# Buffer slots handed out by age, weight splits made one by one, and two small matmuls moved, in a kernel of attention and a feed-forward block

## The chip, the core and the metric

The kernel runs on one core of a Trainium2 chip. The time is that of one execution on the device, in microseconds (us). Engines are named as the profile names them: PE (TensorE, matmuls), PEld (its weight loads), ACT (ScalarE), DVE (VectorE), POOL (GpSimd), and SP, whose queue issues the DMAs.

## The reference

```
xn = layernorm(x)                       # x: 2048 x 512
q, k, v = split(xn @ wqkv)              # 32 heads of 16
p = softmax(q k^T / 4, keys at most 255 behind the query)
s = (p v) @ wo
h = silu(xn @ w1) * (xn @ w3)           # 1792 columns
out = x + s * silu(h @ w2)
```

All inputs and the output are fp32.

## The kernel before, in words

**Precision.** Every dense fp32 product is made of fp16 matmuls. An operand is scaled and split into a high half and a low half (`hi`, `lo`), and a product is the sum of hi·hi, hi·lo and lo·hi. A weight matrix is split in steps: `squares` (L170 on) takes a sum of squares of each part on ACT (`sqa`, L178) or DVE (`sqd`, L180) and casts the sums to `sb` (L190); `powers` multiplies `sb` with ones on PE (L203) and makes a power of two from it on DVE (L205 to L210); the split itself scales the raw weights on ACT (L227), casts the high half on ACT (L228), and subtracts on POOL (L224, in two halves).

**Tiles.** The 2048 tokens are four tiles of 512. For each tile, 4 blocks of 128 tokens are loaded (L317), get their statistics on DVE (bn_stats and bn_aggr, L321 and L322; a 1/sqrt by Newton steps, L326 to L336), are normalised (L339) and transposed on PE (L355) with copies on ACT and DVE (L358, L363).

**Attention.** There are 16 pairs of tile and group of 8 heads, each in two units, so 32 units. `project` makes q or k of a group (L423), `value` makes v (L393). A q or k goes through DRAM (`dQ`, `dK`, L439 to L443) to be fetched in another layout (L455). Pass 1 of a unit (L476 on PE, L481 on DVE) finds the row maxima; they go through DRAM into two more rows of `qa` (L492 to L499). Pass 2 makes the scores (L523), adds masks on DVE (L532, L537), takes the exp on ACT (L541) and multiplies with v (L551). The scores of both passes lie in `s`, two PSUM buffers, so PE can write the next only when DVE or ACT has read the last. `normalise` divides by the sums: POOL multiplies with `rb`, ACT casts the result `O` (L595), POOL subtracts.

**Feed-forward.** F = 1792 is 14 blocks of 128, in four groups. `gate_up` makes the gate and up products of a block (L684), with a tanh on ACT (L695), two products on DVE (L699, L704), and a split of the result `hh` into halves (L708 on ACT, then POOL). `down` (L729) multiplies a group with w2 and adds to an accumulator on DVE (L745). `total` joins attention and feed-forward (sigmoid by a tanh, L765; product L766; output projection L771; store L780). For the first tile the weights are loaded raw (L619 to L621), measured in pairs of blocks (`measure`), split, used, and stored split (`dW1` at L689, `dW2` at L732); the later tiles load the stored halves (L613 to L615).

**What sets the order.** PE's instructions run in the order in which the program emits them; those of the other engines and of SP are ordered by a scheduler that starts from the emission, in which `urgent()` puts softmax work first. The emission is a walk through pieces of dense work: `spread` mixes a unit's batches of attention with dense pieces, and after each piece `step()` raises the count `now` and runs what `later(n, f)` has queued for that count. So `later(4, scale)` is four pieces on. Each engine then runs its instructions in its order, and one that waits holds all behind it.

**Slots.** 32 buffers of SBUF hold raw weights, split weights, q and k on their way, tiles of x, `hh`, accumulators and outputs. `take` pops the first name of a list and `give` appends to its end, when the last use has been emitted. The new user of a slot waits for the last reader of the old one: a matmul, a POOL subtraction, or a DMA that stores it.

The change lies in `take` and `give`, in `measure` and `measure_down`, and in the `give` calls of `project`, `gate_up` and `total`.

Of the kernel before, what the change touches and what calls it, by code (L numbers as in the profile page):

```python
# [11 lines left out]
F16 = mybir.dt.float16  # L12
# [10 lines left out]
D = 512  # L23
# [27 lines left out]
SLOTS = 32  # L51
# [13 lines left out]
def tile_block(ctx: ExitStack, tc: tile.TileContext, x, wqkv, wo, w1, w3, w2, out):  # L65
# [20 lines left out]
    pso = pool("pso", 1, PSUM)  # L86


    free = [f"slot{i}" for i in range(SLOTS)]
    held = {}  # L90

    def take(dtype):
        slot = free.pop(0)
        made = fpool.tile([P, 512 if dtype == F32 else 1024], dtype, name=slot, tag=slot, bufs=1)
        held[id(made)] = slot, made
        return made

    def give(*tiles):
        for made in tiles:
            free.append(held.pop(id(made))[0])  # L100

    queue = []
    now = [0]
    started = []

    def urgent():
# [5 lines left out]
    def later(n, f):  # L115
        made_so_far[0] += 1
        queue.append((now[0] + n, made_so_far[0], f))
# [103 lines left out]
    def halves(op, out, a, b):  # L221

        for c in (slice(0, 256), slice(256, 512)):
            op(out[:, c], a[:, c], b[:, c])  # L224

    def split_pool(hi, lo, raw, s):
        nc.scalar.activation(raw, raw, AF.Copy, scale=s)  # L227
        nc.scalar.copy(hi, raw)  # L228
        halves(nc.gpsimd.tensor_sub, lo, raw, hi)
# [177 lines left out]
    def project(t, g, k, terms=(range(3),)):  # L407


        cell = {}  # L410

        parts = ([[(c, i) for c in (2 * half, 2 * half + 1) for i in range(3)] for half in range(2)] if len(terms) == 1
                 else [[(c, i) for i in group for c in range(NC)] for group in terms])

        def part(n):
            assert turned[t] == 4
            hi, lo, _ = WQK[g]
            xh, xl = X[t]
            if n == 0:
                cell["pp"] = psm.tile([P, TW], F32, name="mm", tag="mm")  # L420
            for c, i in parts[n]:
                a, b = ((hi, xh), (lo, xh), (hi, xl))[i]
                nc.tensor.matmul(cell["pp"], a[:, k, c, :], b[:, c, :], start=(c, i) == parts[0][0],  # L423
                                 stop=(c, i) == parts[-1][-1])
            if n < len(parts) - 1:
                return
            pp = cell["pp"]
            both = take(F16)
            B = both.rearrange("p (a t) -> p a t", a=2)
            s = QS / (XS * WS)  # L430
            with urgent():
                nc.scalar.activation(B[:, 0, :], pp, AF.Copy, scale=s)

            def rest():
                with urgent():
                    nc.vector.scalar_tensor_tensor(B[:, 1, :], pp, s, B[:, 0, :], op0=ALU.mult, op1=ALU.subtract)
                d = (dQ, dK)[k][g][:, :, t * TW:(t + 1) * TW]
                if k == 0:
                    nc.sync.dma_start(d[:, 0:2, :], B[:, 0:1, :].to_broadcast([P, 2, TW]))  # L439
                    nc.sync.dma_start(d[:, 2, :], B[:, 1, :])  # L440
                else:
                    nc.sync.dma_start(d[:, 0:2, :], B)
                    nc.sync.dma_start(d[:, 2, :], B[:, 0, :])  # L443
                give(both)
            later(1, rest)
        return [(len(l), lambda n=n: part(n)) for n, l in enumerate(parts)]

# [155 lines left out]
    WF = {}  # L603
# [21 lines left out]
    def measure(f, apart=0):  # L625

        raws = [RAW[f + i][0] for i in range(2)]
        sb = squares([raws[0][0], raws[1][0], raws[0][1], raws[1][1], RAW[f][1], RAW[f + 1][1]], on_act=4, apart=apart)

        def scale():  # L630
            pp = small.tile([P, 3, 2], F32, name="pp")
            pi = small.tile([P, 3, 2], F32, name="pi")
            powers(sb, 6, pp.rearrange("p a b -> p (a b)"), pi.rearrange("p a b -> p (a b)"))
            ff = slice(f, f + 2)
            nc.vector.tensor_scalar(pi, pi, WS, None, op0=ALU.mult)
            nc.vector.tensor_scalar(sg_scale[:, ff], pp[:, 0, :], 0.5 / (WS * XS), None, op0=ALU.mult)
            nc.vector.tensor_mul(p13[:, ff], pp[:, 0, :], pp[:, 1, :])
            nc.vector.tensor_mul(p132[:, ff], p13[:, ff], pp[:, 2, :])
            measured.update((f, f + 1))

            def cut(i):
                a = [take(F16) for _ in range(2)]
                WF[0, f + i] = [a, None]
                for k in range(2):
                    split_pool(a[k][:, 0:D], a[k][:, D:], raws[i][k], pi[:, k, i:i + 1])
                give(*raws[i])
            later(1, lambda: cut(0))
            later(2, lambda: cut(1))
        later(5 if apart else 4, scale)

    def measure_down(k):

        f0, f1 = GROUPS[k]
        n = f1 - f0
        q = small.tile([P, 1], F32, name="q")
        nc.vector.tensor_reduce(q, p132[:, f0:f1], axis=AX.X, op=ALU.max)
        nc.vector.tensor_scalar(down_scale[:, k:k + 1], q, 1.0 / (HS * WS), None, op0=ALU.mult)
        nc.vector.reciprocal(q, q)
        sw = small.tile([P, 4], F32, name="sw2")
        nc.vector.tensor_scalar(sw[:, 0:n], p13[:, f0:f1], q, WS, op0=ALU.mult, op1=ALU.mult)  # L660

        def cut(f):
            raw2 = RAW.pop(f)[1]
            WF[0, f][1] = b = take(F16)
            split_pool(b[:, 0:D], b[:, D:], raw2, sw[:, f - f0:f - f0 + 1])
            give(raw2)
        assert measured >= set(range(f0, f1))
        for i, f in enumerate(range(f0, f1)):
            later(1 + 2 * i, lambda f=f: cut(f))
# [3 lines left out]
    def gate_up(t, f):  # L673
        cell = {}

        def part(k, half):
            assert turned[t] == 4
            xh, xl = X[t]
            w = WF[t, f][0][k]
            if half == 0:  # L680
                cell[k] = psm.tile([P, TW], F32, name="mm", tag="mm")
            for c in (2 * half, 2 * half + 1):
                for i, (a, b) in enumerate(((0, xh), (1, xh), (0, xl))):
                    nc.tensor.matmul(cell[k], w[:, (a * NC + c) * P:(a * NC + c + 1) * P], b[:, c, :], start=c == 0 and i == 0,  # L684
                                     stop=c == NC - 1 and i == 2)
            if half == 0:
                return
            if t == 0:
                nc.sync.dma_start(dW1[f, k], w)  # L689
            give(w)  # L690
            if k == 0:
                cell["s"] = sg = take(F32)

                with urgent():
                    nc.scalar.activation(sg, cell[0], AF.Tanh, scale=sg_scale[:, f:f + 1])  # L695

                def product():
                    with urgent():
                        nc.vector.scalar_tensor_tensor(sg, sg, 1.0, cell[0], op0=ALU.add, op1=ALU.mult)  # L699
                later(1, product)  # L700
            else:
                sg = cell["s"]
                with urgent():
                    nc.vector.scalar_tensor_tensor(sg, cell[1], 0.5 * HS / (WS * XS)**2, sg, op0=ALU.mult, op1=ALU.mult)  # L704
                HH[t, f] = hh = take(F16)

                def rest():
                    nc.scalar.copy(hh[:, 0:TW], sg)  # L708
                    halves(nc.gpsimd.tensor_sub, hh[:, TW:], sg, hh[:, 0:TW])
                    give(sg)  # L710
                later(1, rest)
        return [lambda k=k, half=half: part(k, half) for k in range(2) for half in range(2)]

    ACC = {}
    XR = {}
# [36 lines left out]
    def total(t, b):  # L752
# [4 lines left out]
        def part(half):  # L757
# [10 lines left out]
            ps, y = cell["ps"], cell["y"]  # L768
# [4 lines left out]
            if half:  # L773
                with urgent():
                    nc.vector.scalar_tensor_tensor(y, ps, sc["y"], y, op0=ALU.mult, op1=ALU.mult)
                if t == NT - 1:
                    nc.vector.tensor_add(y, y, XR[t, b])
                else:
                    halves(nc.gpsimd.tensor_add, y, y, XR[t, b])
                nc.sync.dma_start(out[r, :], y)  # L780
                give(y, XR[t, b])
        return [(6, lambda h=h: part(h)) for h in range(2)]

    def total_by_columns(t, b):
# [51 lines left out]
    tiles = [(t, g) for t in range(NT) for g in range(NG)]  # L836
# [169 lines left out]
    for n in range(len(units)):  # L1006
        t = n // 8
# [12 lines left out]
    for n, u in enumerate(units):  # L1020
# [15 lines left out]
        both = sorted([((i + 0.5) / len(l), k, i) for k, l in enumerate((beside[n], mine)) for i in range(len(l))])  # L1036
        spread(batches(u, units[n + 2] if n + 2 < len(units) else None), [(beside[n], mine)[k][i] for _, k, i in both])
        k = n // 2 + 2
# [42 lines left out]
```

## Time and profile before

| | |
|---|---|
| median of 3 runs | 882.97 us (881.28 to 883.27) |
| profiled execution | 881.5 us |
| span of the profile | 879.6 us |
| ACT, DVE busy | 443.1 us, 626.7 us |
| DMA moved | 110.43 MB |

The span runs from the first to the last recorded instruction; the profiled execution's own time is 1.9 us longer. In the rows of a time line the first column is the start in us, the second the duration, then engine, line, operation and `out<-in`; what stands in brackets is how long the engine stood before it and what ended that. In the rows of the waits stand the waiting and the releasing instruction, then total, times and longest. In the stretches the columns are PE, PEld, DVE, ACT and POOL busy with numbers of instructions, then the granted clock of PE, the DMA share, and GB/s.

### The profile page before, as it was taken

The numbers are of one execution on the slowest core, as the hardware profiler recorded it, in microseconds if no ns is written. First come the engines' busy times: TensorE is split into PE (matmuls) and PEld (weight loads), VectorE is DVE, ScalarE is ACT, GpSimd is POOL, SyncE is SP. The second block draws the span as 40 slices with busy tenths as digits, with TensorE's granted clock in tenths as the row PEclk, the third lists the DMA queues.
The fourth block names the chain that finished last, engine by engine and source line by source line (L and its number), as shares of the span: only waits on it lengthen the run. The fifth ranks groups of instructions, "written<-read, shape, count | busy, mean of one in ns | idle before, by whom it ended". The sixth has DMA issues, their size and how long they took to land.

```text
span 879.6 us, 20432 instructions
## 1 busy us (share of the span) xinstructions
PE 846.5 (96%) x7815; PEld 376.5 (43%) x7815; DVE 626.7 (71%) x1833; ACT 443.1 (50%) x650; POOL 193.9 (22%) x312
## 2 busy tenths in 40 slices
PE   9898898999999999999999999999999999999997
PEld 4333343444444444444444444444444444444443
DVE  8776876877778667787777775776767777666435
ACT  6975877473544444344444445443444444444421
POOL 2254245250201103121110111121111103131211
PEclk9999999999999999999999999999999999999999
DMA  9974534746433353353434344433442253332201
GB/s 293 253 244 148 151 110 126 236 132 222 128 108 70 93 155 107 104 143 98 134 104 103 93 109 135 140 85 104 115 124 84 81 134 115 106 104 82 78 10 59
DMA packets 95073, 110.43 MB, mean 126 GB/s; under 512 B 16960, under 2 KB 60288, under 8 KB 94976
## 3 DMA queue, kind: packets, MB, share of 16 engines
q1 hardware_dynamic: 94688, 108.62, 43.1%
q8 instruction: 61, 1.00, 0.5%
q10 hardware_dynamic: 288, 0.52, 0.2%
q14 instruction: 36, 0.29, 0.1%
HBM read 76.28 MB, written 28.57 MB: 119 GB/s over the span
## 4 chain that ended last, share of the span: by engine, by line
PE 70%; DVE 11%; ACT 5%; issue 4%; DMA 4%; POOL 3%; SPq 2%; POOLq 0%; DVEq 0%; ACTq 0%
PE mm L684 24%; PE mm L729 13%; PE po L551 8%; PE mm L423 6%; PE s L523 6%; PE mm L771 4%; PE s L476 4%; PE mm L393 3%; DVE junk L481 3%; POOL slot L224 2%; DVE s L532 2%; ACT pt L541 1%; DMA slot<-in_A_x_dram 1%; DMA slot<-in_B_w_dram 1%; SPq L590 1%
## 5 line engine op out<-in xcount | busy, mean ns | idle before, releaser
L541 ACT ACTIVATE pt<-s,es 128x1024 f32<-128x1024 f32 (+1 forms) x184 | 200.9, 1093 | 197.5 <-DVE s L532 101.0
L684 PE MATMUL mm<-XH,slot 128*128 128x512 f16 x896 | 268.1, 381 | 0.6 <-POOL slot L224 0.4
L224 POOL TENSOR_TENSOR slot<-slot,slot 128x256 f16<-128x256 f32 (+1 forms) x220 | 146.0, 689 | 529.2 <-ACT slot L708 401.2
L481 DVE CUSTOM_DVE_ANT_0 junk<-s,MW 128x320 bf16<-128x320 f32 x448 | 218.0, 487 | 27.3 <-PE s L476 16.2
L684 PEld LDWEIGHTS <-slot 128*128 128x128 f16 x1344 | 121.6, 98 | 158.9 <-issue 25.2
L684 PE MATMUL mm<-XL,slot 128*128 128x512 f16 x448 | 169.9, 379 | 0.0
L729 PE MATMUL mm<-slot,slot 128*128 128x512 f16 x672 | 160.1, 383 | 0.3
L537 DVE TENSOR_TENSOR s<-s,M 128x512 f32<-128x512 f32 x128 | 89.0, 696 | 62.2 <-PE s L523 53.9
L551 PE MATMUL po<-pt,V 128*32 128x128 f32 (+1 forms) x1920 | 98.3, 330 | 0.0
L729 PEld LDWEIGHTS <-slot 128*128 128x128 f16 x672 | 61.3, 98 | 80.6 <-issue 13.6
L476 PE MATMUL s<-KA,qa 48*64 48x320 f16 (+2 forms) x1024 | 73.6, 298 | 10.7 <-DVE M L481 5.2
L523 PE MATMUL s<-qa,KA 50*64 50x128 f16 (+1 forms) x1920 | 74.2, 251 | 9.9 <-ACT pt L541 6.6
L532 DVE TENSOR_TENSOR s<-s,M 128x1024 f32<-128x1024 f32 x56 | 68.7, 1227 | 15.3 <-PE s L523 13.2
L523 PEld LDWEIGHTS <-KA 50*64 50x64 f16 x1920 | 34.0, 105 | 85.1 <-issue 48.2
L708 ACT CAST slot<-slot 128x512 f16<-128x512 f32 x56 | 34.5, 616 | 61.7 <-DVE slot L704 61.6
L699 DVE SCALAR_TENSOR_TENSOR slot<-slot,mm 128x512 f32<-128x512 f32 x56 | 38.3, 684 | 35.2 <-ACT slot L695 35.1
L551 PEld LDWEIGHTS po<-pt,V 128*32 128x32 f32 x1920 | 49.8, 109 | 24.5 <-issue 11.3
L695 ACT ACTIVATE slot<-mm,sgs 128x512 f32<-128x512 f32 x56 | 38.2, 683 | 31.5 <-PE mm L684 29.8
L224 POOL TENSOR_TENSOR on<-on,rb 128x256 f32<-128x256 f32 x32 | 22.6, 727 | 130.3 <-DMA qa<-dm 50.4
L704 DVE SCALAR_TENSOR_TENSOR slot<-mm,slot 128x512 f32<-128x512 f32 x56 | 38.5, 688 | 17.7 <-PE mm L684 17.6
L745 DVE SCALAR_TENSOR_TENSOR slot<-mm,dsc,slot 128x512 f32<-128x512 f32 x48 | 35.9, 748 | 19.6 <-PE mm L729 19.4
L423 PE MATMUL mm<-XH,whi 128*128 128x512 f16 x128 | 47.2, 381 | 1.3 <-DVE slot L699 0.9
(128 smaller groups left out, 838.3 us busy)
## 6 DMA issues: line engine op xcount, KB each, us to landing
slot<-dW SPq DMA_DIRECT2D x126, 256.0 KB
slot<-in_B_w_dram SPq DMA_DIRECT2D x42, 256.0 KB
dW<-slot SPq DMA_DIRECT2D x42, 256.0 KB
slot<-in_A_x_dram SPq DMA_DIRECT2D x30, 256.0 KB
KA<-dK SPq DMA_DIRECT2D x24, 288.0 KB
qa<-dQ SPq DMA_DIRECT2D x32, 192.0 KB
dK<-slot SPq DMA_DIRECT2D x16, 256.0 KB
dQ<-slot SPq DMA_DIRECT2D x16, 256.0 KB
```

What stands on the lines that cost most here:

```text
L224: op(out[:, c], a[:, c], b[:, c])
L423: nc.tensor.matmul(cell["pp"], a[:, k, c, :], b[:, c, :], start=(c, i) == parts[0][0], stop=(c, i) == parts[-1][-1])
L476: nc.tensor.matmul(s[64 * c:64 * c + 64, r, :n], qa[rows, 2 * p + a, ii * P + 64 * c:ii * P + 64 * c + 64], ka[rows, 2 * p + a, e - n:e], ...
L481: nc.vector.tensor_tensor_reduce(out=junk[:, :n], in0=s[:, r, :n], in1=mask, scale=1.0, scalar=NEG, op0=ALU.add, op1=ALU.max, accum_out=M[ ...
L523: nc.tensor.matmul(s[h:h + 64, r, o:o + w * P], ka[rows, 2 * p + a, (j + 2) * P + h:(j + 2) * P + h + 64], qa[rows, 2 * p + a, q * P:(q + ...
L532: nc.vector.tensor_add(sv, sv, m.unsqueeze(1).to_broadcast([P, 4, 2, P]))
L537: nc.vector.tensor_add(sv[:, :, b, :], sv[:, :, b, :], M2[:, k:k + 1, :].to_broadcast([P, 4, P]))
L541: nc.scalar.activation(pt[:, :, 0:n], s.rearrange("p r (a q) -> p (r a) q", a=2)[:, :, 0:n], AF.Exp, scale=es)
L551: nc.tensor.matmul(cell["po"][32 * i:32 * i + 32, q * P:(q + w) * P], V[:, (4 * t + j) % VB, h * VW:h * VW + 32], pt[:, i, o:o + w * P], s ...
L684: nc.tensor.matmul(cell[k], w[:, (a * NC + c) * P:(a * NC + c + 1) * P], b[:, c, :], start=c == 0 and i == 0, stop=c == NC - 1 and i == 2)
L704: nc.vector.scalar_tensor_tensor(sg, cell[1], 0.5 * HS / (WS * XS)**2, sg, op0=ALU.mult, op1=ALU.mult)
L729: nc.tensor.matmul(ps, hh[:, a * TW + b * P:a * TW + (b + 1) * P], w[:, c * D:(c + 1) * D], start=f == f0 and i == 0, stop=f == f1 - 1 and ...
```

## The change

A slot that is given back carries the count at which it counts as free: `now`, plus 4 to 6 pieces if its last reader is POOL or a store. `take` hands out the slot with the lowest count, in place of the first in the list. The splits of w1 and w3 of a pair of blocks, two at a time before, each get a due time of their own (1, 2, 4 and 6 pieces on), and each raw slot is given back at once. Before the attention units begin, the product with ones in `measure` comes 6 pieces on in place of 4, or 9 in place of 5; after that it stays at 5.

```
-    free = [f"slot{i}" for i in range(SLOTS)]
+    now = [0]
+    free = [(0, i, f"slot{i}") for i in range(SLOTS)]
     held = {}
+    given = [SLOTS]
     def take(dtype):
-        slot = free.pop(0)
+        free.sort()
+        slot = free.pop(0)[2]
...
-    def give(*tiles):
+    def give(*tiles, after=0):
         for made in tiles:
-            free.append(held.pop(id(made))[0])
+            given[0] += 1
+            free.append((now[0] + after, given[0], held.pop(id(made))[0]))
...
-                give(both)
+                give(both, after=4)
...
-            def cut(i):
-                a = [take(F16) for _ in range(2)]
-                WF[0, f + i] = [a, None]
-                for k in range(2):
-                    split_pool(a[k][:, 0:D], a[k][:, D:], raws[i][k], pi[:, k, i:i + 1])
-                give(*raws[i])
-            later(1, lambda: cut(0))
-            later(2, lambda: cut(1))
-        later(5 if apart else 4, scale)
+            def cut(i, k):
+                if k == 0:
+                    WF[0, f + i] = [[None, None], None]
+                WF[0, f + i][0][k] = a = take(F16)
+                split_pool(a[:, 0:D], a[:, D:], raws[i][k], pi[:, k, i:i + 1])
+                give(raws[i][k], after=5)
+            for i in range(2):
+                for k in range(2):
+                    later((1, 2, 4, 6)[2 * i + k], lambda i=i, k=k: cut(i, k))
+        later(5 if started else 9 if apart else 6, scale)
...
-            give(raw2)
+            give(raw2, after=5)
...
-            give(w)
+            give(w, after=4 * (t == 0))
...
-                    give(sg)
+                    give(sg, after=4)
...
-                give(y, XR[t, b])
+                give(y, XR[t, b], after=6)
```

More of the change, by code (lines that the diff above doesn't have):

```diff
@@ L96, in take @@
         return made
-    def give(*tiles):
+    def give(*tiles, after=0):
         for made in tiles:
-            free.append(held.pop(id(made))[0])
+            given[0] += 1
+            free.append((now[0] + after, given[0], held.pop(id(made))[0]))
     queue = []
-    now = [0]
     started = []
```

## The prediction

> **What bounds the kernel now.** I read the page's busy times and slices first, then the waits of TensorE (PE), then the stretches, and last the time line around each gap that the change can reach.
>
> ```profile
> PE 846.5 (96%) x7815; PEld 376.5 (43%) x7815; DVE 626.7 (71%) x1833; ACT 443.1 (50%) x650; POOL 193.9 (22%) x312
> ...
> PE   9898898999999999999999999999999999999997
> ```
>
> PE is busy for 846.5 of 879.6 us, so the change, which leaves the number of PE's instructions as it is, can win at most the 33 us in which PE stands. The slices with less than nine tenths lie in the first seven (0 to 154 us) and at the end. The waits of PE, grouped by what released it (total, times, longest):
>
> ```profile
> PE s L523 <- ACT pt L541: 6.6, 8, 1.6
> PE s L476 <- DVE M L481: 5.2, 8, 1.1
> PE s L476 <- ACT pt L541: 3.5, 3, 2.2
> PE ps L203 <- DVE sb L190: 2.9, 3, 1.6
> ```
>
> These four rows hold 18.2 us. All but the last are waits for a bank of scores, `s`, which ScalarE (ACT) or VectorE (DVE) has not yet read; none is a wait for a slot by PE itself. Slots enter at one remove: an in-order engine that waits for a slot is late with the softmax work queued behind it. The stretches, each with PE, PEld, DVE, ACT and POOL busy:
>
> ```profile
> 60.00:80.00 20.00, 17.93 (x148) 7.77 (x149) 13.21 (x47) 12.74 (x21) 12.03 (x19) 1.00 0.42 140
> 80.00:100.00 20.00, 15.88 (x119) 6.31 (x119) 16.18 (x64) 11.75 (x20) 8.04 (x13) 0.91 0.51 148
> 100.00:125.00 25.00, 25.00 (x222) 11.06 (x221) 18.38 (x67) 17.21 (x31) 5.15 (x8) 1.00 0.33 95
> ...
> 160.00:180.00 20.00, 18.99 (x161) 7.95 (x159) 18.56 (x71) 10.19 (x19) 3.27 (x7) 1.00 0.73 234
> ...
> 190.00:400.00 210.00, 205.71 (x1969) 90.86 (x1965) 154.79 (x450) 95.73 (x128) 36.88 (x56) 1.00 0.45 129
> 400.00:870.00 470.00, 464.10 (x4499) 206.68 (x4492) 319.78 (x843) 209.59 (x267) 81.30 (x122) 1.00 0.36 99
> ```
>
> After 190 us PE stands for 4.3 us and 5.9 us; from 60 to 100 us alone for 6.2 us, with the granted clock at 1.00 and 0.91. So the early stretch has the most to give. But from 160 to 180 us DVE is busy for 18.56 of 20 us: there an instruction put earlier on DVE delays every one behind it.
>
> **The change, part by part.** The changed program has the same instructions. PE's order differs in two places only, the two products with ones; ACT's, DVE's, the queue of DMAs' (SP) and a few of GpSimd's (POOL) orders differ in some hundreds of places, by the new slots and due times.
>
> *The two products.* The rows are PE's wait for the product of measure(0), the matmul behind it, the last accumulator read of the squares on ACT, and PE's wait for the product of `qk[2]`.
>
> ```profile
> 29.29 0.17 PE L203 MATMUL ps<-sb,onesb 128*128 128x6 bf16 x1 [1.13 <-DVE sb L190]
> 29.71 0.38 PE L393 MATMUL mm<-wvh,XH 128*128 128x512 f16 x1 [0.26 <-DVE al L205]
> 33.56 0.20 ACT L178 ACTIVATION_READ_ACCUMULATOR sqa<-slot 128x1 f32 x1
> 34.01 0.19 PE L203 MATMUL ps<-sb,onesb 128*128 128x1 bf16 x2 [1.55 <-DVE sb L190]
> ```
>
> The change moves the first product behind value(1), just ahead of the one at 34.01. The gaps of 1.13 and 0.26 us go, so PE reaches 34.01 some 1.4 us sooner; but that product needs squares whose last ends on ACT at 33.76, and ACT's squares stand in an unchanged order. What is late next is the same `sb`: the wait grows by what was saved. I put this at 0. The bounds are a gain of 1.4 (ACT earlier by as much) and a loss of 0.5 (the splits behind both products, which wait for their scale, start later).
>
> *Splits one by one, slots by age, 58 to 76 us.* First ACT and DVE, then PE.
>
> ```profile
> 61.26 0.62 ACT L228 CAST slot<-slot 128x512 f16<-128x512 f32 x1 [2.27 <-PE mm L684]
> ...
> 64.55 0.62 ACT L228 CAST slot<-slot 128x512 f16<-128x512 f32 x1 [1.41 <-POOL slot L224]
> ...
> 66.89 0.62 ACT L228 CAST slot<-slot 128x512 f16<-128x512 f32 x1 [1.14 <-PE mm L684]
> ```
>
> ```profile
> 65.78 0.69 DVE L699 SCALAR_TENSOR_TENSOR slot<-slot,mm 128x512 f32<-128x512 f32 x1 [1.21 <-ACT slot L695]
> ```
>
> ```profile
> 59.44 0.33 PE L476 MATMUL s<-KA,qa 48*64 48x320 f16 x4 [1.14 <-DVE M L481]
> 68.16 0.25 PE L476 MATMUL s<-KA,qa 48*64 48x128 f16 x4 [0.81 <-PE s L523]
> ...
> 75.25 0.39 PE L684 MATMUL mm<-XH,slot 128*128 128x512 f16 x1 [0.36 <-POOL slot L224]
> ```
>
> Two casts of the splits of w2 wait 2.27 and 1.41 us for a slot just given back. With slots by age, both take slots that were given back before their turn comes, and the waits go. The third (66.89) still takes one that a matmul of L684 frees, so its wait stays. The tanh L695 behind the second cast comes some 2 us sooner, DVE's L699 with it, and the row maxima L481 behind L699 no longer hold the scores: the 0.81 at 68.16 goes, some 0.4 of the 1.14 at 59.44, and about 0.3 of the 0.36 for a split at 75.25. Sum: 0.81 + 0.4 + 0.3 = **+1.5**; bounds 0 (the third cast holds the rest) and 2.3 (all three gaps).
>
> *76 to 100 us.*
>
> ```profile
> 80.30 0.69 DVE L321 BATCH_NORM_STATS2 st<-slot 128x6 f32<-128x512 f32 x1 [2.29 <-DMA slot<-in_A_x_dram]
> ```
>
> ```profile
> 81.38 0.30 PE L476 MATMUL s<-KA,qa 48*64 48x256 f16 x4 [1.00 <-DVE M L481]
> 89.36 0.33 PE L476 MATMUL s<-KA,qa 48*64 48x320 f16 x4 [2.18 <-ACT pt L541]
> 98.95 0.25 PE L476 MATMUL s<-KA,qa 48*64 48x128 f16 x4 [0.72 <-DVE M L481]
> ```
>
> DVE stands 2.29 us in bn_stats for a load of x, with row maxima queued behind; PE's 1.00 at 81.38 follows from it. In the changed order that bn_stats stands behind those maxima, so the 1.00 goes. Of the 2.18 I take 0.5, of the 0.72 0.3: **+1.8**. Against it, two of the four loads of x take slots that POOL frees later, and a sum of squares of w2 (L180) moves ahead of a maximum and waits for its load. Bounds: −1.0 (that wait, at most the 2.29 shown, shows on PE by half) and 3.9 (all three gaps).
>
> *100 to 155 us.* Sums of squares of the next weights move ahead of two mask additions (L537); tanh L695 moves ahead of a copy; the cast of a normalised head, L595, moves ahead of a transposed tile's copy and waits for POOL's product.
>
> ```profile
> L180 DVE CUSTOM_DVE_ANT_0 sqd<-slot x20: 679/686/1121, 17.8 to 207.6; 128x512 bf16<-128x512 f32 x20
> ```
>
> ```profile
> L224 POOL TENSOR_TENSOR on<-on,rb x2: 724/726/729, 146.9 to 147.6; 128x256 f32<-128x256 f32 x2
> ```
>
> ```profile
> 134.75 0.30 PE L476 MATMUL s<-KA,qa 48*64 48x256 f16 x4 [1.12 <-ACT pt L541]
> ```
>
> Two sums at 0.69 put 1.4 on the path at most, of which I take 0.5, since DVE is not full there. The copy behind L595 waits for two products of 0.73 us, 1.45; I take 0.6. The gap of 1.12 goes but for 0.3 (+0.8). Sum **−0.3**, bounds −2.9 and +1.1.
>
> *160 to 181 us.* The bn_stats of the next tile, their 1/sqrt chain and three of its four normalisations move ahead of mask additions, maxima and gate products on the full DVE.
>
> ```profile
> L321 DVE BATCH_NORM_STATS2 st<-slot 128x6 f32<-128x512 f32 x4 | 2.7, 677 | 0.0
> L339 DVE TENSOR_SCALAR slot<-slot,mv,rs 128x512 f32<-128x512 f32 x4 | 2.2, 545 | 0.0
> ```
>
> ```profile
> 161.40 1.12 DVE L180 CUSTOM_DVE_ANT_0 sqd<-slot 128x512 bf16<-128x512 f32 x1 [1.20 <-DMA slot<-in_B_w_dram]
> ```
>
> ```profile
> 176.47 0.38 PE L423 MATMUL mm<-XH,whi 128*128 128x512 f16 x1 [0.90 <-DVE slot L699]
> ```
>
> Three bn_stats stand ahead of one mask addition: 3 × 0.68 = 2.0 us late for exp and PE. The three normalisations ahead of the gate product at 176 add 3 × 0.55 = 1.6 at a place where PE already waits 0.90. Of this 3.6, the 1.20 us wait for a weight load shrinks by about 1 (two DMAs of that pair go ahead of a stalled store), and dense work covers some 0.8. I take **−1.8**; bounds −4.5 (all of it and the 0.90 again) and +0.9 (all covered, and the 0.90 gone).
>
> *After 190 us.* First ACT, then PE.
>
> ```profile
> 344.40 0.63 ACT L765 ACTIVATE slot<-slot 128x512 f32<-128x512 f32 x1 [3.92 <-DMA out_dram<-slot]
> ```
>
> ```profile
> 318.78 0.33 PE L476 MATMUL s<-KA,qa 48*64 48x320 f16 x4 [0.89 <-PE s L523]
> 346.08 0.41 PE L523 MATMUL s<-qa,KA 50*64 50x256 f16 x8 [1.37 <-ACT pt L541]
> 403.42 0.42 PE L523 MATMUL s<-qa,KA 50*64 50x128 f16 x16 [1.16 <-ACT pt L541]
> ```
>
> ACT waits 3.92 us for the slot of a store and the exp behind it is late; in the changed order that exp stands first, which takes about 1.2 of the 1.37, and a like wait before 318.78 gives 0.4. Against these, near 572 us the sigmoid L765 moves ahead of an exp and would wait for a store, and near 739 us another waits for POOL: I take −0.8, near half of the two gains. Sum **+0.8**; bounds −2 and +2.8 (all three gaps, less the losses).
>
> **Sum:** 0 + 1.5 + 1.8 − 0.3 − 1.8 + 0.8 = 2.0 us sooner. The profiled execution took 881.5 us (span 879.6 and 1.9 around it), so 879.5. The runs' median, 882.97, lies 1.5 above it, within their spread of 881.28 to 883.27; from it the forecast is **881.0**.
>
> [...]
>
> **The rivals.**
> (a) *Slower.* Work for the next tile, put ahead of softmax work on the in-order DVE, is paid whole: −4.5 for −1.8 from 160 to 181 us, and the same from 76 to 100 us, where the moved sum waits for its load, takes back the +1.8. That decides if the instruction held up is the one that PE waits for, with no dense work left before it. Then 2.0 − 2.7 − 1.8 = −2.5 us: 885.5. For it: 18.56 of 20 us busy. Against it: PE waited only 0.90 us there before, and its order puts dense matmuls between any two sets of scores.
> (b) *No change.* What 58 to 100 us gives (3.3) is handed back at the next wait whose releaser did not move, as at 34.01. Of the losses of 2.1 from 100 to 181 us, 1.0 then falls into the same waits: 2.0 − 3.3 + 1.0 = −0.3 us, 883.3. Against it: from 100 to 125 us PE is busy for 25.00 of 25 us, so a shift passes through.
> (c) *Much faster.* The moved DVE work is covered (0 for −1.8) and the 1.16 at 403 us goes, where the next tile's statistics move back: 2.0 + 1.8 + 1.2 = 5.0 us sooner, 878.0.
> [...]
> That the change does not do what it says has no chance of its own: the changed order shows the two casts with other slots.
>
> **How the numbers follow.** Forecast 0.38, its own range 879.5 to 882.5; (a) 0.27, (b) 0.17, (c) 0.13, (d) 0.05. A measurement of this kernel can tell about 0.2%, 1.8 us, from no change. Faster (below 881.2) gets (c), 0.26 of the forecast and 0.07 of (b) and (d), whose unknown costs reach both ways: 0.46. Within 0.2% (881.2 to 884.7): 0.12 of the forecast, 0.13 of (b) and (d), 0.02 of (a): 0.27. Slower: 0.25 of (a) and 0.02 of (b): 0.27. The range, 876.5 to 886.5, takes in (c) and (a), with 1.5 and 1.0 us beyond for the bounds of the terms; the bounds all at one end would reach farther and are left out.
>
> **What would show it.** Right: PE's waits from 58 to 100 us fall by 3 us or more, casts L228 no longer wait for slots at 61 and 64 us, no bn_stats stands for a load with maxima behind it at 80 us, the wait near 34 us grows to about 2.9 us, and PE stands some 2 us longer from 160 to 181 us. Wrong: a wait near 34 us below 2 us (ACT's squares came sooner), gaps from 160 to 181 us above 4 us (a), or a new wait of DVE or ACT for a load or store of over 2 us with PE behind it.

## The result and the profile after

| | kernel before | changed kernel |
|---|---|---|
| median | 883.59 us (20 executions, 881.09 to 885.83) | 880.31 us (20 executions, 876.73 to 884.60) |
| ratio | | 0.9967, 95% interval 0.9954 to 0.9980 |
| profiled execution | 881.5 us, mean granted clock 0.997 | 881.87 us, mean granted clock 0.994 |

The change makes the kernel 3.3 us faster (0.3%). But the profiled execution of the changed kernel is no shorter than that of before, and its executions spread over 7.9 us, where those of before spread over 4.7. Both facts come mainly from PE's granted clock. The page shows busy times first, then that clock by slices.

```profile
PE 849.4 (97%) x7815; PEld 377.2 (43%) x7815; DVE 624.6 (71%) x1833; ACT 443.0 (50%) x650; POOL 193.7 (22%) x312
...
PEclk9999899999999999999999999999999999999999
```

PE waits less (span less busy time: 33.1 us before, 30.5 now) but is busy for 2.9 us more with the same 7815 matmuls: some of them ran at a lower clock. PE's waits in the changed kernel, whose lines have moved by 4 to 5:

```profile
PE s L480 <- DVE M L485: 7.1, 8, 3.6
PE s L527 <- DVE M L485: 3.7, 10, 0.5
PE ps L207 <- DVE sb L194: 3.5, 2, 3.3
PE s L480 <- ACT pt L545: 3.0, 4, 2.0
PE s L527 <- ACT pt L545: 2.0, 5, 0.5
```

The waits for exps (ACT pt) fell from 10.1 to 5.0 us. The longest wait for maxima (DVE M) rose from 1.1 to 3.6 us, and the wait for the product with ones is one of 3.25. On the time line of PE:

```profile
34.21 0.19 PE L207 MATMUL ps<-sb,onesb 128*128 128x1 bf16 x2 [3.25 <-DVE sb L194]
...
87.27 0.33 PE L480 MATMUL s<-KA,qa 48*64 48x320 f16 x4 [2.00 <-ACT pt L545]
...
98.07 0.32 PE L480 MATMUL s<-KA,qa 48*64 48x128 f16 x4 [3.57 <-DVE M L485]
```

Stretches of 3 us behind two of these waits (PE, PEld, DVE, ACT, POOL busy, then the granted clock):

```profile
33.00:36.00 3.00, 1.79 (x16) 0.84 (x16) 1.78 (x15) 3.00 (x8) 0.00 (x0) 0.95 0.96 232
36.00:39.00 3.00, 3.00 (x9) 1.06 (x8) 1.98 (x4) 1.68 (x4) 1.85 (x2) 0.50 0.91 169
...
96.00:99.00 3.00, 0.93 (x6) 0.42 (x7) 2.65 (x13) 1.17 (x3) 0.69 (x1) 0.69 0.98 331
99.00:102.00 3.00, 3.00 (x8) 1.06 (x7) 2.51 (x19) 1.87 (x3) 0.00 (x0) 0.50 0.36 96
102.00:105.00 3.00, 3.00 (x28) 1.20 (x27) 1.02 (x2) 1.63 (x5) 0.00 (x0) 0.67 0.52 139
```

Behind both long waits PE runs at 0.50: from 36 us on, the matmuls of one product start 0.43 us apart (36.01, 36.43, 36.86), where a microsecond earlier they start 0.21 apart (35.01, 35.22, 35.44). The kernel before has one such stretch, behind its wait of 2.18 us at 89 us:

```profile
90.00:93.00 3.00, 3.00 (x11) 1.07 (x12) 2.27 (x15) 2.36 (x4) 1.02 (x3) 0.50 0.32 87
```

To see where time went, I took the starts of the same matmul in both traces. The table gives how much later (+) or earlier (−) it starts after the change:

| start before, us | 34 | 38 | 59 | 76 | 94 | 99 | 103 | 115 | 158 | 186 | 311 | 351 | 431 | 872 |
|---|---|---|---|---|---|---|---|---|---|---|---|---|---|---|
| difference, us | +0.2 | +1.8 | +0.9 | −0.5 | −3.7 | −0.9 | +1.9 | +2.7 | +2.0 | +2.3 | +2.3 | +0.4 | −0.1 | +0.3 |

So 1.6 us are lost by the clock behind 34 us, 5.5 are won up to 94 us, and 5.6 are lost again at 98 to 103 us, half by the wait and half by the clock behind it; after 186 us another 2 are won. Of the 5.5, the last 1.6 (from −2.1 at 89 us to −3.7 at 94) are not the work of a shorter wait: they are the half-speed stretch at 90 us, which the traced execution of the kernel before paid and that of the changed kernel did not.

How often the clock drops differs between executions, and it orders the times. Executions at the same mean granted clock:

| mean granted clock | before, beside the experiments | changed kernel |
|---|---|---|
| 0.998 | 880.08 to 883.55 (26) | 876.73 to 878.65 (3) |
| 0.996 | 882.96 to 884.18 (15) | 878.05 to 881.30 (4) |
| 0.994 | 884.61 to 885.45 (3) | 880.00 to 881.87 (4) |

At one clock the changed kernel is some 4 us ahead. Part of that it gives back because its clock is more often low: 0.994 in the median, against 0.998 for the 58 executions of the kernel before that ran beside the experiments. How much is not known exactly: the clocks of the 20 executions of the kernel before in the first table are not on record. Executions at one clock still differ by up to 3.5 us, which the clock does not explain.

### The profile page after: what moved, and what is told of

It reads as the page before. It is cut to its first block, busy times and chain, and to the rows that moved or that the text cites. A ratio compares the mean times of both kernels' runs of the same rounds, so it can differ in the third digit from the quotient of the medians.

```text
span 879.9 us, 20423 instructions
## 1 busy us (share of the span) xinstructions
PE 849.4 (97%) x7815; PEld 377.2 (43%) x7815; DVE 624.6 (71%) x1833; ACT 443.0 (50%) x650; POOL 193.7 (22%) x312
## 4 chain that ended last, share of the span: by engine, by line
PE 61%; DVE 10%; DMA 6%; ACT 5%; issue 5%; POOL 3%; SPq 3%; POOLq 0%; DVEq 0%; ACTq 0%
PE mm L689 22%; PE mm L734 12%; PE po L555 7%; PE s L527 5%; PE mm L427 5%; PE mm L776 4%; DVE junk L485 3%; PE s L480 3%; PE mm L397 3%; POOL slot L228 3%; DVE s L536 2%; ACT pt L545 1%; SPq L594 1%; DMA slot<-in_B_w_dram 1%; DMA de<-dr 1%
## 5 line engine op out<-in xcount | busy, mean ns | idle before, releaser
L734 PEld LDWEIGHTS <-slot 128*128 128x128 f16 x672 | 61.5, 99 | 81.8 <-issue 14.9
```

The costliest lines, as they stand in the source:

```text
L734: nc.tensor.matmul(ps, hh[:, a * TW + b * P:a * TW + (b + 1) * P], w[:, c * D:(c + 1) * D], start=f == f0 and i == 0, stop=f == f1 - 1 and ...
```

## Experiments

The question: is the clock the price of the two long waits (theory A throughout), or do the waits cost only themselves? And which part of the change wins the time? A ratio is the time over that of the kernel before.

**The products alone** (kernel before).

```
-        later(5 if apart else 4, scale)
+        later(5 if started else 9 if apart else 6, scale)
```

> The kernel before, with the two products with ones moved as in the change and nothing else. Theory A (clock): joining the waits at 29.29 and 34.01 us into one wait of about 3 us leaves PE's standing as it was, but that long a wait lowers PE's granted clock to 0.50 for about 3 us, so matmuls take 0.43 us each in place of 0.21: about 1.6 us slower than before. Rival B (waits only): the sum of the two waits is unchanged, so no difference (within 0.5 us) and no clock below 1.00 near 36 us.

Measured: ratio 1.0018 (1.0001 to 1.0035), 884.52 us against 882.54. The wait was 3.26 us. In the profiled execution no clock fell and it took 881.06 us; the 12 executions took 880.94 to 888.03 us, with mean clocks from 1.000 (881.06 us) down to 0.991 (886.95 us). At equal clock the two kernels agree (at 0.998: 880.94 to 883.55 us, against 880.08 to 883.55), so what the moved products cost is the clock. A holds for the median, with a correction: a wait of 3.26 us does not lower the clock every time. In that trace the clock stood at 1.00 from 33 to 42 us.

**Filling the wait at 34 us** (changed kernel).

```
     run(value(1))
+    keep_busy(12)
     qk[2][2]()
```

> The changed kernel, with 12 matmuls of ones put on PE in the wait at 34 us; their product is used nowhere. Theory A (clock): PE's wait there falls from 3.25 to about 0.7 us, the end of it stays where it was (34.2 us), the clock stays at 1.00, and the kernel is about 1.6 us faster than the changed one, so about 4.5 to 5 us faster than before. Rival B (the matmuls behind 35.6 us are slow for another reason): no gain, about 3 us faster than before as the change alone, and matmuls of 0.43 us at 36 to 39 us stay.

Measured: ratio 0.9958 (0.9943 to 0.9972), 3.7 us faster than before, where A had 4.5 to 5. The wait was 0.22 us, its end stayed at 34.0 us, and the clock stayed up:

```profile
36.00:39.00 3.00, 3.00 (x23) 1.21 (x21) 2.23 (x3) 3.00 (x7) 1.85 (x3) 1.00 1.17 222
```

B is out: with PE standing 0.22 us in place of 3.25, no matmul from 36 to 39 us was slowed. At 38 us PE was 1.9 us ahead of the changed kernel. But part of it was handed on to the next wait with a fixed end, 3.12 us where it had been 2.00, and behind that the clock fell to 0.50 (87 to 90 us):

```profile
86.70 0.48 PE L480 MATMUL s<-KA,qa 48*64 48x320 f16 x4 [3.12 <-ACT pt L545]
```

**The sum of squares at 95 us behind the maxima** (changed kernel). On DVE that sum stood ahead of the maxima for which PE waited at 98 us:

```profile
94.98 1.18 DVE L184 CUSTOM_DVE_ANT_0 sqd<-slot 128x512 bf16<-128x512 f32 x1 [3.43 <-DMA slot<-in_B_w_dram]
```

```
+                sums.append(i)
-                nc.vector.tensor_tensor_reduce(out=sq, ...)
+                with tc.issue_after(maxima[47].ins) if len(sums) == 11 else nullcontext():
+                    nc.vector.tensor_tensor_reduce(out=sq, ...)
```

`maxima` holds the row maxima in the order in which they are emitted, and `issue_after` queues what follows behind one of them on its engine. The code of this edit and of the next ones of its kind is shown shortened: the kernels look the positions up in small tables.

> The changed kernel, with one sum of squares of w2 (the one at 94.98 us that waited 3.43 us for its load) queued on DVE behind the two row maxima that stood behind it. Theory A (DVE order and clock): PE's wait of 3.57 us at 98 us falls below 1 us and the clock stays at 1.00 from 96 to 105 us: 2.8 us by the wait and 2.8 us by the clock, about 5.5 us faster than the changed kernel, 8 us faster than before. Rival B (the load itself, not its place on DVE, holds PE): the wait moves to the next user, the gain is below 1 us. Rival C (wait only): 2.8 us, with the slow matmuls left.

Measured: ratio 0.9940 (0.9927 to 0.9952), 877.69 us. The wait of 3.57 us went, one of 1.20 came at the next scores, and the clock stayed at 1.00:

```profile
98.00 0.42 PE L527 MATMUL s<-qa,KA 50*64 50x128 f16 x16 [1.20 <-DVE M L485]
```

```profile
99.00:102.00 3.00, 3.00 (x15) 1.35 (x14) 2.65 (x10) 2.52 (x7) 0.00 (x0) 1.00 0.83 262
```

At 103 us PE was 5.4 us ahead of the profiled execution of the changed kernel, where 5.5 was expected; 0.5 of that it had at 94 us already, ahead of the edit. In the median the gain is 0.9940 against 0.9967, some 2.4 us, and 5.3 us against the kernel before, where A had 8: that profiled execution had paid more than most.

**Both edits.**

> The changed kernel with both edits: 12 unused matmuls of ones in the wait at 34 us, and the one sum of squares behind the two row maxima at 95 us. Theory A: the two gains add, 1.6 + 5.5 = 7 us faster than the changed kernel, about 10 us faster than before, with a mean granted clock of 0.998 or more. If the rivals hold: 3 to 6 us faster than before.

Measured: ratio 0.9948 (0.9933 to 0.9963): no better than the sum alone, so the gains did not add. The wait at 87 us was 3.63 us here. That wait ends by a load: ahead of the mask addition two bn_stats stood 2.39 and 1.27 us on DVE for tiles of x, and what PE wins ahead of it is lost in it.

**Slots by age alone, and splits one by one alone** (kernel before, with the `take`, `give` and `after=` lines of the change, or with its `cut` alone).

> The kernel before with the slots taken by age (with the later counts for POOL and the stores) and nothing else: no splits one by one, products with ones where they were. Theory A (the gain from 58 to 94 us comes from slots that ACT's casts no longer wait for): the casts of w2 near 61 and 64 us do not wait for slots, PE is ahead by 2 us or more at 94 us, and the kernel is 2 to 3 us faster than before. Rival B (it comes from the splits one by one, which leave the slots free in time): under 1 us by slots alone.

> The kernel before with the splits of w1 and w3 one by one, each raw slot given back at once, and nothing else: slots in the order of return, products with ones where they were. Theory A (the slots make the gain): within 1 us of before. Rival B (the splits make it): 2 to 3 us faster than before and PE ahead by 2 us or more at 94 us.

Measured: ratio 0.9975 (0.9964 to 0.9985) for the slots, 0.9967 (0.9955 to 0.9980) for the splits. By time both parts pay, 2.2 and 2.9 us; the whole change, moved products included, wins 3.3, so they do not simply add. Lead of PE against before:

| start before, us | 59 | 68 | 76 | 85 | 94 | 99 | 103 | 311 | 351 | 872 |
|---|---|---|---|---|---|---|---|---|---|---|
| slots by age alone | 0.3 | 0.3 | 0.3 | 1.7 | 0.7 | 0.7 | 0.7 | −0.1 | 1.9 | 2.2 |
| splits one by one alone | 0.3 | 1.4 | 1.7 | 3.1 | 5.3 | 6.2 | 2.4 | 0.9 | 1.1 | 1.4 |

The gain from 59 to 76 us is the splits' (B). With the slots alone the casts still waited, 1.79 and 1.69 us, against A. From 76 to 85 us either part alone gives the same 1.4. What the slots then lose at 89 us is a wait of 3.30 us, and of the splits' lead at 94 us 1.6 are again the half-speed stretch of the kernel before. The splits alone also lose at 98 us (a wait of 2.50 us, then the clock), though there DVE stood 3.76 us in a bn_stats and not in a sum of squares. The slots by age win after 311 us.

**The change without its moved products.**

> The changed kernel with the two products with ones put back to where they were before. Theory A (clock): two waits of about 1.1 and 1.5 us near 29 and 34 us in place of one of 3.25, so the clock is 1.00 from 33 to 42 us in every record, and the time is 1 to 1.6 us below that of the changed kernel, about 4 to 5 us faster than before. Rival B (the position of the products does not matter): about 3 us faster than before, as the change.

Measured: ratio 0.9952 (0.9937 to 0.9968), 878.38 us. In the profile the two waits are 1.13 and 1.55 us, and the clock is 1.00 from 20 to 96 us; behind the wait at 98 us, 3.6 us here, it falls as in the changed kernel. The medians favour A; the interval of the change itself (0.9954 to 0.9980) overlaps with this one.

**Statistics behind softmax work as well** (changed kernel, with the sum behind the maxima). At 84 us the first bn_stats waited ahead of the mask addition whose exp PE needs at 87 us:

```profile
83.95 0.69 DVE L325 BATCH_NORM_STATS2 st<-slot 128x6 f32<-128x512 f32 x1 [2.14 <-DMA slot<-in_A_x_dram]
```

```
-            nc.vector.bn_stats(st, xts[b])
+            seen.append(b)
+            with tc.issue_after(masks[4].ins) if len(seen) in (5, 6) else nullcontext():
+                nc.vector.bn_stats(st, xts[b])
```

> The changed kernel with two edits of DVE's order: the sum of squares of w2 behind the two row maxima near 95 us, and the first two bn_stats of the next tile, of which the first waited 2.14 us for its load at 84 us, behind the mask addition at 85.81 us. Theory A (work for the next tile, ahead of softmax work on the in-order DVE, holds PE): PE's waits of 2.00 us at 87 us and of 3.57 us at 98 us both fall below 1 us, no granted clock below 1.00 after 42 us, 7 to 8 us faster than the changed kernel, 10 us faster than before. Rival B (the load is needed soon after anyway): the wait at 87 us is only passed on to a later bank of scores, and the kernel is no faster than with the first edit alone (about 5 us faster than before).

Measured: ratio 0.9907 (0.9890 to 0.9924), 874.53 us against 882.96: 8.2 us by the ratio, where A had 10. The wait at 87 us is gone, and no clock fell after 42 us; but part of it was passed on, as B had it, to a wait further on:

```profile
93.82 0.25 PE L482 MATMUL s<-KA,qa 48*64 48x128 f16 x4 [2.38 <-DVE M L487]
```

**All three edits: products back, sum and statistics behind.**

> The changed kernel with three edits: the two products with ones back where they were before, the sum of squares of w2 behind the row maxima near 95 us, the first two bn_stats of the next tile behind a mask addition near 85 us. Theory A: the effects add, 1.3 us for the products (by the run that moved them alone, ratio 1.0018) on top of 0.9907 for the other two edits: ratio about 0.989, 9 to 10 us faster than before, no wait of PE over 2.5 us after 20 us, mean granted clock 0.998 or more in nearly all executions. Rival B (what PE wins ahead of 42 us is passed on to a wait for a load near 94 us): no better than 0.9907.

Measured: ratio 0.9896 (0.9881 to 0.9912), 873.71 us against 882.39: 8.7 us by the medians, 9.2 by the ratio. The four executions had clocks of 0.998 to 1.000. This version beats both kernels. The last step, from 0.9907, lies within the intervals.

**The fourth bn_stats behind, too** (the kernel with three edits).

```
-            with tc.issue_after(masks[4].ins) if len(seen) in (5, 6) else nullcontext():
+            with tc.issue_after(masks[4 if len(seen) < 8 else 5].ins) if len(seen) in (5, 6, 8) else nullcontext():
```

> The kernel with all three edits (products back, sum of squares and first two bn_stats of the next tile behind softmax work), and the fourth bn_stats, which waited 1.67 us for its load at 91 us ahead of two row maxima, behind the mask addition that follows them. Theory A (work for the next tile, ahead of softmax work, holds PE): PE's wait of 2.29 us at 93 us falls below 1 us, and the kernel is 1.5 to 2 us faster than with three edits, about 11 us faster than before (ratio 0.987 to 0.988). Rival B (the transposes of the next tile then come late, since the statistics' chain ends later): PE waits as long for L359 near 130 us, ratio 0.9896 or more.

Measured: ratio 0.9887 (0.9870 to 0.9903), 873.69 us: the same within the interval. The wait of 2.29 us at 93 us went, and one of 2.67 came at the next exp. On ACT it has the same pattern: a sum of squares that waits for its load, ahead of that exp.

```profile
92.94 0.63 ACT L183 ACTIVATE sqa<-slot 128x512 bf16<-128x512 f32 x1 [2.53 <-DMA slot<-in_B_w_dram]
```

```profile
96.54 0.25 PE L482 MATMUL s<-KA,qa 48*64 48x128 f16 x4 [2.67 <-ACT pt L547]
```

Neither theory had it: the transposes near 130 us waited 0.68 us, as they did without the edit.

**Output slots free at once** (changed kernel).

```
-                give(y, XR[t, b], after=6)
+                give(y, XR[t, b])
```

> The changed kernel with the output slots counted as free at once, not 6 pieces later. Theory A (the gain at 319 and 346 us comes from ACT no longer waiting for the slot of a store ahead of an exp): the wait of ACT's sigmoid for the store comes back near 340 us, PE loses 1 to 1.5 us there, and the kernel is 1 to 1.5 us slower than the changed one (about 1.5 to 2 us faster than before). Rival B (age alone, without the later count, does it): as the changed kernel, about 3 us faster than before.

Measured: ratio 0.9955 (0.9939 to 0.9972), no slower than the change. The mechanism is there: ACT waits for the store again, with the exp behind it. First this kernel, then the changed one, where the exp comes first:

```profile
344.51 0.63 ACT L770 ACTIVATE slot<-slot 128x512 f32<-128x512 f32 x1 [3.06 <-DMA out_dram<-slot]
345.05 1.10 ACT L545 ACTIVATE pt<-s,es 128x1024 f32<-128x1024 f32 x1
```

```profile
345.09 1.11 ACT L545 ACTIVATE pt<-s,es 128x1024 f32<-128x1024 f32 x1 [2.80 <-DVE s L536]
346.11 0.62 ACT L770 ACTIVATE slot<-slot 128x512 f32<-128x512 f32 x1
```

PE's wait that returns is 0.51 us, not 1 to 1.5; so small a loss does not show in the time. A's size was wrong.

**The clock by itself** (kernel before with 20 waits put in).

```
+    def hold(k):
+        z = small.tile([P, P], BF16, name="z", bufs=1)
+        ps = [psm.tile([P, P], F32, name="ps", tag="mm") for _ in range(2)]
+        nc.tensor.matmul(ps[0], onesb, onesb, start=True, stop=True)
+        with urgent():
+            nc.scalar.copy(z, ps[0])
+            for i in range(k):
+                nc.scalar.copy(z, z)
+        nc.tensor.matmul(ps[1], onesb, z, start=True, stop=True)
...
+        if 8 <= n < 28:
+            hold(6 + (n - 8) // 2)
```

> The kernel before with 20 waits put in, one at each unit from the ninth on: an unused matmul, a chain of 7 to 16 small copies on ACT, and an unused matmul that reads their end, so that PE stands some 1.5 to 4 us each time, at moments that have no relation to each other. [...] Rival B (the early dips have to do with the loads at the start): no granted clock below 1.00 behind any of them. The time itself is longer by the waits, 50 us or more.

Measured: 999.6 us, one execution. Five of the 20 waits of PE, and the 10 us around them:

```profile
273.50 0.26 PE L946 MATMUL ps<-z,onesb 128*128 128x128 bf16 x1 [2.33 <-ACT z L945]
...
302.38 0.22 PE L946 MATMUL ps<-z,onesb 128*128 128x128 bf16 x1 [2.72 <-ACT z L945]
...
356.14 0.26 PE L946 MATMUL ps<-z,onesb 128*128 128x128 bf16 x1 [4.05 <-ACT z L945]
...
475.43 0.27 PE L946 MATMUL ps<-z,onesb 128*128 128x128 bf16 x1 [3.32 <-ACT z L945]
...
505.76 0.26 PE L946 MATMUL ps<-z,onesb 128*128 128x128 bf16 x1 [3.65 <-ACT z L945]
```

```profile
271.00:281.00 10.00, 7.67 (x58) 3.23 (x57) 5.76 (x18) 5.17 (x11) 0.53 (x1) 0.83 0.07 16
300.00:310.00 10.00, 7.62 (x63) 3.34 (x62) 4.07 (x11) 5.12 (x10) 1.29 (x2) 1.00 0.31 88
...
354.00:364.00 10.00, 7.86 (x51) 3.01 (x51) 4.58 (x11) 4.15 (x9) 1.30 (x2) 0.66 0.18 45
...
474.00:484.00 10.00, 8.57 (x54) 3.31 (x54) 4.41 (x11) 4.17 (x8) 0.00 (x0) 0.66 0.02 5
504.00:514.00 10.00, 8.24 (x63) 4.01 (x63) 6.03 (x15) 5.43 (x11) 0.00 (x0) 0.83 0.19 60
```

Ten microseconds at 0.83 are 1.7 us short of full clock, at 0.66 3.4 us. Over all 20 waits the shortfall has three sizes only: 0 (two waits, 2.66 and 2.72 us), about 1.7 (eight) and about 3.4 us (ten). That is as much as 0, 3.4 or 6.8 us at half clock. Every wait of 2.99 us or more (17 of them) was followed by one of the two losses; of the three shorter ones, 2.33, 2.66 and 2.72, only the shortest was. So length does not decide alone, and B, the loads at the start, is out: the drops come from 273 to 851 us.

Such stretches stand in the traces of the two kernels as well: until the last 1.1 us of the span, the clock of the kernel before was at 0.50 from 90.01 to 93.43 us, that of the changed kernel from 35.72 to 39.14 and from 97.16 to 103.99, so for 3.4 us twice and for 6.8 us once. The joined wait of the two products shows both cases at one length. Behind the 3.25 us of the changed kernel the clock was at 0.50 from 36 to 39 us (the row stands with its time line above); behind the 3.26 us of the kernel with the products alone it stayed at 1.00:

```profile
33.00:36.00 3.00, 1.92 (x18) 0.98 (x18) 1.90 (x16) 3.00 (x8) 0.00 (x0) 1.00 0.94 230
36.00:39.00 3.00, 3.00 (x22) 1.22 (x21) 2.19 (x5) 3.00 (x7) 1.77 (x3) 1.00 0.95 237
```

What decides in place of the length is not shown here.

## Why the prediction was right, and where it was not

The forecast was 2.0 us faster, and the measured gain is 3.3 (0.33%, interval 0.20% to 0.46%). The sign is right; the terms are right only in part, and the clock is missing from all of them. In the traced executions they come to 0.3 us later (+0.3 at 872 us), not 2.0 earlier. That the median lands near the forecast is partly luck: what went wrong from 34 to 38 us and from 76 to 103 us, which not every execution need pay in full, stands against the last two terms, which came out 2.7 better than forecast.

- **The two products, 0.** The wait grew to 3.25 us, as said (2.9), and its end stayed. But the step "I put this at 0", with a loss of at most 0.5, failed: behind the single long wait the clock was at 0.50 for 3.4 us (35.72 to 39.14), at the cost of 1.6 us by 38 us. From 38 to 59 us PE won 0.9 back, of which no term spoke. Moved alone, the products cost 1.6 us (1.0018). The dip to 0.91 from 80 to 100 us was quoted and not priced.
- **58 to 76 us, +1.5.** From 59 to 76 us PE won 1.4 us. The size is right, the reason not: the splits one by one did it, not the slots by age, and the casts did not stop waiting. In the changed order the tanh stands ahead of the waiting cast:

```profile
62.11 0.62 ACT L232 CAST slot<-slot 128x512 f16<-128x512 f32 x1 [0.67 <-PE mm L689]
...
64.65 0.69 ACT L700 ACTIVATE slot<-mm,sgs 128x512 f32<-128x512 f32 x1 [0.86 <-PE mm L689]
67.79 0.62 ACT L232 CAST slot<-slot 128x512 f16<-128x512 f32 x1 [2.46 <-PE mm L689]
```

- **76 to 100 us, +1.8.** Up to 94 us 3.2 were won, half by shorter waits and 1.6 because the kernel before ran at 0.50 behind its wait of 2.18 us, a price that the prediction did not count. Then the sum of squares stood ahead of the maxima, as was said, but it waited 3.43 us, more than the 2.29 taken as the most, and showed on PE not by half but whole: PE lost 2.8 by the wait and 2.8 by the clock. In the profiled execution the term is −2.4, outside its bounds; rival (a) had named just this for the stretch, but at 1.8 us for the whole. A bn_stats still stood for its load at 84 us, ahead of a mask addition rather than of maxima, so the sign to look for, no bn_stats with maxima behind it, was met in the letter and PE still waited 2.00 us.
- **100 to 155 us, −0.3.** From 103 to 158 us 0.1 was lost, 0.8 up to 115 us and 0.7 won back. The net is right.
- **160 to 181 us, −1.8.** Only 0.3 was lost (+2.0 at 158, +2.3 at 186). The order had changed as said, but PE's matmuls covered the work: the longest waits there are 0.61 and 0.41 us, and PE stands 1.3 us in all, against 1.0 before. The term was too large, and this place of rival (a) falls.

```profile
169.70 0.33 PE L480 MATMUL s<-KA,qa 48*64 48x320 f16 x4 [0.61 <-DVE M L485]
...
178.70 0.38 PE L427 MATMUL mm<-XH,whi 128*128 128x512 f16 x1 [0.41 <-DVE slot L704]
```

- **After 190 us, +0.8.** 2.0 were won: 2.0 at 319 and 346 us and 0.9 more up to 632 us, less 0.8 near 740 us; near 572 us nothing was lost. The gains were put too low. In the bounds, the three gaps less the losses are 3.42 − 0.8 = 2.6, not 2.8; nothing else rests on it.
- **Rivals.** (b), handing on a gain, does occur: filling the wait at 34 us showed it at 87 us. It did not undo the change. (d), slower sums of squares on DVE, did not occur: no run shows its term of 1.7 us, and the 20 sums took 15.2 us before and 14.9 after.

```profile
L184 DVE CUSTOM_DVE_ANT_0 sqd<-slot 128x512 bf16<-128x512 f32 x20 | 14.9, 756 | 5.8 <-DMA slot<-in_B_w_dram 5.7
```

- **Its own signs.** Of those for right, the wait near 34 us and the order at 80 us came; but PE stands 7.3 us from 58 to 100 us as before, not 3 less, the casts still wait, and from 160 to 181 us PE does not stand 2 us longer. One of those for wrong came too: a new wait of DVE for a load of over 2 us (3.43) with PE behind it. So up to 181 us the change did not win in the way that was forecast; behind 190 us it did, by the exp that no longer stands behind the wait for a store.

The profiled executions alone (881.87 us against 881.5) would have spoken for no change; the medians and the comparison at one clock speak for 3 to 4 us. What stays open is what share of executions pays at 34 us and what share at 98 us: only one trace of each kernel exists, and the mean clock of the others does not say where it fell.

## What to carry to other kernels

Price a wait of TensorE by its length as well as by its place: of the 20 waits put in, all 17 of 2.99 us or more and one of the three shorter were followed by 3.4 or 6.8 us at half clock, a further price of 1.7 or 3.4 us. Two waits joined into one of 3.25 us so cost 1.6 us in one trace; in another, a joined wait of 3.26 us left the clock at 1.00. On an in-order engine, work for a later stage that waits for a load must not stand ahead of softmax work; queueing two statistics and one sum of squares behind it, with the products left where they were, took the gain from 0.3% to 1.0%. Compare executions at the same granted clock before believing one trace.

## What was not expected of the hardware

PE's clock fell to 0.50 for 3.4 or 6.8 us at a time: behind a wait of 2.18 us in the kernel before, and behind all 17 of the put-in waits from 2.99 us on. It did not fall behind put-in waits of 2.66 and 2.72 us, nor behind the wait of 3.26 us in the profiled execution of the kernel with the products alone. What makes the difference is not known here, so a wait's length does not say whether it pays, and the mean clocks of that kernel's 12 executions go from 0.991 to 1.000.
